# Window attention and a softplus FFN on one core: which block runs while weights are still being converted, and which engine scales the second head

## The chip, the cores and the metric

One core of a Trainium2 chip runs the whole kernel as one program. The metric is the device time of one execution in microseconds (us). The engines of the core work side by side, each through its own instructions in order: TensorE (PE in the profile; PEld is its weight loads), VectorE (DVE), ScalarE (ACT), GpSimd (POOL), and SyncE (SP), which issues all of this kernel's transfers.

## The reference

Eight sequences of 576 tokens, eight heads of 64. Each query sees itself and the 63 tokens before it; the result, 4608 tokens of 512, goes through an FFN with softplus between its two products. All is float32.

```python
scores = scale * np.matmul(q, k.transpose(0, 1, 3, 2))
rel = pos[:, None] - pos[None, :]
scores = np.where((rel >= 0) & (rel < 64), scores, -1e9)
attn = np.exp(scores - np.max(scores, axis=-1, keepdims=True))
attn = attn / (np.sum(attn, axis=-1, keepdims=True) + 1e-09)
x = np.matmul(attn, v)            # heads side by side: 4608 x 512
h = x @ w_in                      # 512 x 2048
g = np.maximum(h, 0.0) + np.log1p(np.exp(-np.abs(h)))
out = g @ w_out                   # 2048 x 512
```

## The kernel before

**Tiling.** The tokens are cut into 12 blocks of 384 (TB), numbered g in the order in which they run (ORDER: first the two blocks that begin a sequence at a block's edge and come first, then the rest). The 2048 middle columns of the FFN are cut into 16 weight tiles f of 128. An FFN *step* is one (g, f): `ffn_up` makes 128 columns of h for the block with 12 matmuls, three ScalarE operations (L454 to L456) and up to three more (L458 to L461) make softplus of it, and `ffn_down` adds its product to the block's three output tiles in ps_o with 9 matmuls. Operands are split into a high and a low float32r part, and each product is made of three.

**Weights.** The weights arrive as float64. `load_w(f)` fetches the two halves of tile f, w_in's and w_out's, and `float64_split` turns the words into a high and a low part: on DVE L162 to L165, on ScalarE L161 and L166, on POOL L167 (and L162 for the first four half tiles). Both parts stay in SBUF for the rest of the run. Tiles 8 to 15 lie in "spare" space that the attention of blocks 0 and 1 uses first.

**Attention.** `attention(g, hp)` handles one pair of heads of one block as a chain of stages, a Python generator. For g < 2 the transposes of q and k are made by TensorE, in float32. For the other blocks q and k are split into bf16 parts in `nat` (L309 to L313), transposed by DMA into `tr` (L314), and multiplied (L334). Then for each 128 tokens come mask and minimum on DVE (L342), exponential with its sum on ScalarE (L345), reciprocal of the sum (L352, L353) and the scaling of the probabilities by it (L358), for both heads; then transposes by TensorE (L379, L380), the product with v (L427) and x, in a high and a low part, in tiles `x{i}_{hp}_{side}`. `nat`, `tr`, `xf` and `vt` exist once, so one pair at a time is in each stage. There are two sets of x tiles: blocks 0 and 1 have one each, and the later blocks take turns, block 2 with the set of block 1.

**Order.** `passes` lists which block runs over which weight tiles: block 0 over tiles 0 to 7 (SPLIT), block 1 over all 16, block 0 over the rest, then each other block over all 16. Where a block stops in between, its sums are written to DRAM (`spill`, the tensor `part`), and when its second pass ends they are fetched and added (`fill`). Everything is put into one list of events, sorted by a number: step n has its first half at 2n + 0.5 and its second at 2n + 3.5, so two units are a step; a pair of heads has its stages at a base plus the offsets in STG0 (blocks 0 and 1), STG2 (block 2) or STG, the base being BASE[g] + PACE[g] * hp for the first three blocks. `load_w(f)` stands 12 units (AHEAD) ahead of the first step that uses f. This list is what the program is traced from. From event 100 on, TensorE's order is that of the list; ahead of it, and on the other engines throughout, a scheduler orders instructions ahead of time, the earlier in the list the sooner where several could go.

Of the kernel before, what the change touches and what calls it, by code (L numbers as in the profile page):

```python
# [8 lines left out]
F32 = mybir.dt.float32  # L9
BF16 = mybir.dt.bfloat16  # L10
F32R = mybir.dt.float32r
U32 = mybir.dt.uint32
AF = mybir.ActivationFunctionType
ALU = mybir.AluOpType

P = 128
TB = 384
# [3 lines left out]

SPLIT = 8
AHEAD = 12
BASE = (-100, -46, 2 * (SPLIT + 16) - 24)
PACE = (5, 5, 4)
STG0 = (-8, 1, 3, 4, 5, 7, 8, 9, 10)
STG2 = (-8, 0, 2, 3, 4, 6, 7, 8, 9)
STG = (-13, -5, 0, 0, 3, 5, 7, 8, 11)
# [8 lines left out]
def window_attention_softplus_ffn(  # L37
# [16 lines left out]
    nc = tc.nc  # L54
    B, H, S, D = q.shape
    NT, DM = out.shape
    DF = w_in.shape[1]
    NP = H // 2
    NC = DM // P
    NF = DF // P  # L60
    NB = NT // TB
# [9 lines left out]
    xp = ctx.enter_context(tc.tile_pool(name="xp", bufs=1))  # L71
    ff = ctx.enter_context(tc.tile_pool(name="ff", bufs=2))
    late = ctx.enter_context(tc.tile_pool(name="late", bufs=1))
    dram = ctx.enter_context(tc.tile_pool(name="dram", bufs=1, space=bass.MemoryType.DRAM))
# [42 lines left out]
    def weight(m, i, f):  # L117

        if f < NE:
            return w_first[m][i][:, f, :]  # L120
        k = (f - NE) // 4
        if (m, i, k) not in w_last:
            w_last[m, i, k] = spare(4 * k + 2 * m + i, [P, 4, DM], F32R, f"w{m}{i}{k}")
        return w_last[m, i, k][:, f % 4, :]
# [19 lines left out]
    def raw_tiles(f):  # L144

        ks = (5,) if f < NE else [k for k in (5,) if k >= 4] if f < NE + 4 else []
        at = f % (len(ks) + 1)
        if at == len(ks):
            return [ff.tile([P, NC, P], w_in.dtype, name="raw", bufs=2) for _ in range(2)]
        t = spare(ks[at], [P, 2, NC, P], w_in.dtype, "raws")  # L150
        return [t[:, m, :, :] for m in range(2)]
# [17 lines left out]
    def load_w(f):  # L169
        fs = slice(f * P, (f + 1) * P)  # L170
        raws = raw_tiles(f)
        for m, src in enumerate((w_in[:, fs].rearrange("(c p) n -> p c n", p=P), w_out[fs, :].rearrange("p (c n) -> p c n", n=P))):
            hi, lo = [weight(m, i, f).rearrange("p (c n) -> p c n", n=P) for i in range(2)]
            float64_split(hi, lo, src, raws[m], 2 * f + m)
# [55 lines left out]
    xs = {}  # L230
    taken_ps = [0]

    def attention(g, hp):
# [6 lines left out]
        def bank():  # L240
            if not odd0:
                return ps_a.tile([P, 512], F32, name="ps_a")

            taken_ps[0] += 1
            return ps_o.tile([P, 512], F32, name=f"ps_o{taken_ps[0] % NJ}")
# [27 lines left out]
        if by_pe:  # L273
# [17 lines left out]
            for hh in range(2):  # L291
                rows = slice(hh * D, (hh + 1) * D)
# [29 lines left out]
        rs = att.tile([P, NJ, 2], F32, name="rs", bufs=2)  # L322
        for j in range(NJ):
            first = j == 0 and not prev
            c0 = WIN if first else 0
            n = W - c0
            sp = bank()
            spv = sp[:, : 2 * n].rearrange("p (h c) -> p h c", h=2)
            kc = slice(j * P + WIN + c0, (j + 2) * P)
            if by_pe:  # L330
                mm(spv, qt[:, j * P : (j + 1) * P], kbd[:, :, j * P + c0 : j * P + W], start=True, stop=True)
            for hh in range(0 if by_pe else 2):
                for i, (a, b) in enumerate(((0, 0), (0, 1), (1, 0))):
                    mm(  # L334
                        spv[:, hh, :], tr_q[a][:, hh, j * P : (j + 1) * P], tr_k[b][:, hh, kc],
                        start=(hh == 0 and i == 0), stop=(hh == 1 and i == 2), skip_group_check=True,
                    )
            t = ORDER[g] * NJ + j
            m = mask_b if (t * P) % S + P > S else mask
            for hh in range(2):  # L340
                pv = p_t[hh][:, j, WIN + c0 :]
                nc.vector.tensor_tensor_reduce(  # L342
                    pv, spv[:, hh, :], m[:, c0:], 1.0, 3.0e38, ALU.add, ALU.min, mn[:, j, hh : hh + 1]
                )
                nc.scalar.activation(  # L345
                    pv, pv, AF.Exp, bias=mn[:, j, hh : hh + 1], scale=-1.0, accum_out=sm[:, j, hh : hh + 1]
                )
            if by_pe and j < NJ - 1:
                yield
                continue  # L350
            jr = slice(0, NJ) if by_pe else slice(j, j + 1)
            nc.vector.tensor_scalar(rs[:, jr, :], sm[:, jr, :], 1.0e-9, None, ALU.add)  # L352
            nc.vector.reciprocal(rs[:, jr, :], rs[:, jr, :])  # L353
            for jj in range(jr.start, jr.stop):
                for hh in range(2):
                    c0 = WIN if jj == 0 and not prev else 0
                    pv = p_t[hh][:, jj, WIN + c0 :]
                    nc.vector.tensor_scalar(pv, pv, rs[:, jj, hh : hh + 1], None, ALU.mult)  # L358
            yield


# [27 lines left out]

        if hp == 0:  # L390
            xs[g] = [[None] * NP, [None] * NP]
        side = 0 if g == 0 else 1 if g == 1 else (g + 1) % 2
        x_t = [xp.tile([P, TB], F32R, name=f"x{i}_{hp}_{side}") for i in range(2)]
        for i in range(2):
            xs[g][i][hp] = x_t[i]
        if by_pe:
# [3 lines left out]
        for hh in range(2):  # L400
# [6 lines left out]
            for kb in reversed(range(NJ)):  # L407
                n = W if kb < NJ - 1 else P
# [26 lines left out]
            yield  # L435


    gs = {}
    ops = {}
    part = {}  # L440
# [23 lines left out]
    def ffn_down(g, f, first, last):  # L464
        gt = gs.pop((g, f))
        if first:
            ops[g] = [ps_o.tile([P, DM], F32, name=f"ps_o{j}") for j in range(NJ)]
        for j in range(NJ):
            js = slice(j * P, (j + 1) * P)
            for i, (a, b) in enumerate(((0, 0), (0, 1), (1, 0))):  # L470
                mm(  # L471
                    ops[g][j], gt[a][:, js], weight(1, b, f),
                    start=(first and i == 0), stop=(last and i == 2),
                )
        if last:
            rows = out[ORDER[g] * TB : (ORDER[g] + 1) * TB, :]
            spill, fill = f < NF - 1, f == NF - 1 and g in part
            if spill:
                part[g] = rows = dram.tile([TB, DM], F32, name="part")
            for j0, j1 in ((0, 2), (2, 3)):  # L480
                o = ff.tile([P, NC, P], w_in.dtype, name="raw", bufs=2).bitcast(F32)
                o = o.rearrange("p c n -> p (c n)").rearrange("p (j n) -> p j n", n=DM)[:, : j1 - j0, :]
                rs = slice(j0 * P, j1 * P)
                if fill:
                    nc.sync.dma_start(o, part[g][rs, :].rearrange("(j p) n -> p j n", p=P))
                for j in range(j0, j1):
                    if fill:
                        nc.vector.tensor_tensor(o[:, j - j0, :], o[:, j - j0, :], ops[g][j], ALU.add)
                    else:
                        (nc.scalar.copy if j == 1 else nc.vector.tensor_copy)(o[:, j - j0, :], ops[g][j])  # L490
                nc.sync.dma_start(rows[rs, :].rearrange("(j p) n -> p j n", p=P), o)
# [2 lines left out]

    passes = [(0, 0, SPLIT), (1, 0, NF), (0, SPLIT, NF)] + [(g, 0, NF) for g in range(2, NB)]
    steps = [(g, f, f == f0, f == f1 - 1) for g, f0, f1 in passes for f in range(f0, f1)]


# [2 lines left out]
    events = []  # L503
    for g in range(NB):
        for hp in range(NP):
            if g < 3:
                base = BASE[g] + PACE[g] * hp
            else:
                base = 2 * NF * (g - 1) + SHP * hp + SH
            stages = attention(g, hp)  # L510
            for at in STG if g >= 3 else STG2 if g >= 2 else STG0:
                events.append((base + at, lambda stages=stages: next(stages, None)))
    loaded = 0
    for n, (g, f, first, last) in enumerate(steps):
        if f == loaded:
            events.append((2 * n - AHEAD, lambda f=f: load_w(f)))
            loaded += 1
        events.append((2 * n + 0.5, lambda g=g, f=f: ffn_up(g, f)))
        events.append((2 * n + 3.5, lambda step=steps[n]: ffn_down(*step)))
    events.sort(key=lambda e: e[0])  # L520
    for at, emit in events:
        if at < PE_ORDERED_FROM:
# [34 lines left out]
```

## Time and profile before

| | us |
|---|---|
| median of 3 runs | 1072.06 (1069.83 to 1072.11) |
| the profiled execution | 1069.74 |
| its span, first to last instruction | 1067.9 |
| PE busy | 1028.4 (96%) |
| DVE busy | 789.0 (74%) |
| ACT busy | 650.0 (61%) |
| POOL busy | 224.7 (21%) |
| mean share of the 16 DMA engines (hardware queue) | 40.0% |
| TensorE clock granted, of full speed | 0.993 |

Each row of the profile's groups stands for all instructions of one source line, engine and operation: count, busy time, mean ns of one, and the idle time of the engine just before them with what ended it. A row of tenths cuts the span into 40 slices of 26.7 us. L358 is line 358 of the kernel before. Busy time of PE is not PE at its peak, since matmuls overlap.

### The profile page before, as it was taken

To read this page: it belongs to the slowest core of one execution; us is meant where nothing else is said; L and a number is where in the kernel's file an instruction comes from. 1 tells how busy PE (TensorE), PEld (TensorE's weight loads), DVE (VectorE), ACT (ScalarE), POOL (GpSimd) and SP (SyncE) were. 2 spreads that over 40 slices of the span, in tenths; PEclk is the share of its full clock that TensorE was granted. 3 is DMA by queue.
4 is the path that set the end of the run, shared out by engine and by line. 5 is a ranking of instruction groups with operands and counts; after the bars stand their busy time and mean duration, and the time that the engine had idled before them with its cause. 6 is when DMAs were issued, how large, how long until landed. Compare 5 with 4: busy or idle time off the path is not lost.

```text
span 1067.9 us, 18172 instructions
## 1 busy us (share of the span) xinstructions
PE 1028.4 (96%) x6096; PEld 924.3 (87%) x6096; DVE 789.0 (74%) x2319; ACT 650.0 (61%) x1669; POOL 224.7 (21%) x217
## 2 busy tenths in 40 slices
PE   7797988999999999999999999999999999999998
PEld 5576867888999899999999999999999999999996
DVE  4999899866777777777777777777777777865433
ACT  6786666666665666566656666656666665655333
POOL 4354355631111111112111111111211111110000
PEclk9999998999999999999999999999999999999999
DMA  7754645255334434343344334424434533520000
GB/s 197 198 140 105 169 105 146 67 127 119 70 71 101 96 79 105 64 97 81 81 96 96 84 76 93 107 60 88 102 74 84 115 80 62 131 51 1 30 1 30
DMA packets 296222, 98.20 MB, mean 92 GB/s; under 512 B 280512, under 2 KB 288704, under 8 KB 296128
## 3 DMA queue, kind: packets, MB, share of 16 engines
q1 hardware_dynamic: 296128, 97.03, 40.0%
q8 instruction: 48, 0.79, 0.3%
q14 instruction: 46, 0.38, 0.1%
HBM read 50.07 MB, written 10.22 MB: 56 GB/s over the span
## 4 chain that ended last, share of the span: by engine, by line
PE 78%; DVE 12%; DMA 4%; ACT 3%; issue 2%; SPq 1%; POOL 0%; DVEq 0%; ACTq 0%
PE ps_h L450 32%; PE ps_o L471 31%; PE ps_a L334 5%; PE ps_a L427 4%; PE ps_a L380 2%; DMA tr<-nat 2%; PE ps_a L379 2%; DVE p_t L358 2%; DVE osb L165 2%; DVE osb L164 1%; DVE osb L162 1%; DVE p_t L342 1%; DVE osb L163 1%; SPq L198 1%; DVE u L458 1%
## 5 line engine op out<-in xcount | busy, mean ns | idle before, releaser
L450 PE MATMUL ps_h<-x,w 128*128 128x384 f32 x2304 | 458.4, 344 | 15.4 <-DVE u L458 11.8
L471 PE MATMUL ps_o<-w,g 128*128 128x512 f32 x1728 | 438.7, 397 | 6.3 <-ACT g L460 4.3
L450 PEld LDWEIGHTS ps_h<-x,w 128*128 128x128 f32 x2304 | 400.6, 189 | 27.5 <-DVE u L458 12.5
L471 PEld LDWEIGHTS ps_o<-w,g 128*128 128x128 f32 x1728 | 318.1, 188 | 65.6 <-ACT g L460 4.6
L458 DVE SCALAR_TENSOR_TENSOR u<-ps_h,u 128x384 f32<-128x384 f32 x192 | 106.0, 552 | 139.7 <-ACT u L456 139.5
L454 ACT ACTIVATE u<-ps_h 128x384 f32<-128x384 f32 x192 | 93.6, 488 | 179.4 <-PE ps_h L450 177.2
L345 ACT ACTIVATE p_t<-p_t,mn 128x192 f32<-128x192 f32 (+1 forms) x288 | 127.0, 443 | 63.5 <-DVE mn L342 63.2
L140 POOL TENSOR_TENSOR x<-xf,x 128x384 fp32r<-128x384 f32 x40 | 41.1, 1027 | 460.6 <-DVE rs L352 362.9
L358 DVE TENSOR_SCALAR p_t<-p_t,rs 128x192 f32<-128x192 f32 (+1 forms) x288 | 110.4, 429 | 2.9
L342 DVE CUSTOM_DVE_ANT_0 p_t<-ps_a,mask 128x192 f32<-128x192 f32 (+1 forms) x244 | 77.3, 343 | 46.5 <-PE ps_a L334 36.1
L455 ACT ACTIVATE u<-u 128x384 f32<-128x384 f32 x192 | 100.7, 526 | 4.1
L456 ACT ACTIVATE u<-u 128x384 f32<-128x384 f32 x192 | 100.6, 524 | 3.2
L461 DVE TENSOR_TENSOR g<-u,g 128x384 fp32r<-128x384 f32 x160 | 89.5, 559 | 3.8 <-DVE g L460 0.5
L385 ACT CAST pt<-ps_a 128x512 fp32r<-128x512 f32 (+1 forms) x144 | 59.0, 417 | 33.7 <-PE ps_a L380 21.9
L312 POOL TENSOR_TENSOR nat<-q_in,nat 128x384 bf16<-128x384 f32 x40 | 38.6, 965 | 187.8 <-ACT nat L311 152.1
L386 DVE TENSOR_TENSOR pt<-ps_a,pt 128x512 fp32r<-128x512 f32 (+1 forms) x144 | 67.9, 477 | 12.3 <-ACT pt L385 10.7
L334 PE MATMUL ps_a<-tr 128*128 128x192 bf16 (+1 forms) x720 | 74.8, 246 | 0.9 <-DVE xf L432 0.7
L460 DVE CAST g<-u 128x384 fp32r<-128x384 f32 x176 | 67.9, 386 | 5.9
L380 PE MATMUL ps_a<-ident,p_t 128*128 128x128 f32 x276 | 66.6, 276 | 1.4 <-DVE p_t L358 1.3
L427 PEld LDWEIGHTS ps_a<-pt,vt 128*128 128x128 f32 (+1 forms) x608 | 64.0, 163 | 3.9 <-issue 0.5
L427 PE MATMUL ps_a<-pt,vt 128*128 128x64 f32 (+4 forms) x608 | 64.5, 247 | 0.4 <-DVE mn L342 0.4
L431 ACT COPY xf<-ps_a 64x384 f32<-64x384 f32 x80 | 38.1, 477 | 40.3 <-PE ps_a L427 37.5
(91 smaller groups left out, 1019.3 us busy)
## 6 DMA issues: line engine op xcount, KB each, us to landing
out_dram<-raw SPq DMA_DIRECT2D x12, 512.0 KB, 3.2
q_in<-in_q_dram SPq DMA_DIRECT2D x56, 96.0 KB, 2.6
raw<-in_moe_w_in_dram SPq DMA_DIRECT2D x10, 512.0 KB, 4.2
raw<-in_moe_w_out_dram SPq DMA_DIRECT2D x10, 512.0 KB, 4.2
k_in<-in_k_dram SPq DMA_DIRECT2D x32, 128.0 KB, 3.5
v_in<-in_v_dram SPq DMA_DIRECT2D x32, 128.0 KB, 2.8
raws<-in_moe_w_in_dram SPq DMA_DIRECT2D x6, 512.0 KB, 4.2
raws<-in_moe_w_out_dram SPq DMA_DIRECT2D x6, 512.0 KB, 5.0
```

Source lines behind the costliest of these rows:

```text
L334: mm(spv[:, hh, :], tr_q[a][:, hh, j * P : (j + 1) * P], tr_k[b][:, hh, kc], start=(hh == 0 and i == 0), stop=(hh == 1 and i == 2), skip_g ...
L342: nc.vector.tensor_tensor_reduce(pv, spv[:, hh, :], m[:, c0:], 1.0, 3.0e38, ALU.add, ALU.min, mn[:, j, hh : hh + 1])
L345: nc.scalar.activation(pv, pv, AF.Exp, bias=mn[:, j, hh : hh + 1], scale=-1.0, accum_out=sm[:, j, hh : hh + 1])
L358: nc.vector.tensor_scalar(pv, pv, rs[:, jj, hh : hh + 1], None, ALU.mult)
L427: mm(av[: D if lo else P, osl], vt[:, vb, hh, : 1 if lo else 2, :], pt[hh][lo][:, psl], start=(i == 0), stop=(i == len(order) - 1), skip_g ...
L450: mm(hv, weight(0, a, f)[:, c * P : (c + 1) * P], x[b][c], start=(i_mm == 0), stop=(i_mm == 3 * NC - 1))
L454: nc.scalar.activation(u, hv, AF.Abs)
L455: nc.scalar.activation(u, u, AF.Exp, scale=-1.0)
L456: nc.scalar.activation(u, u, AF.Ln, bias=1.0)
L458: nc.vector.scalar_tensor_tensor(gf, hv, 0.0, u, ALU.max, ALU.add)
L461: (nc.vector if g >= 2 else nc.gpsimd).tensor_tensor(gt[1], gf, gt[0].bitcast(F32), ALU.subtract)
L471: mm(ops[g][j], gt[a][:, js], weight(1, b, f), start=(first and i == 0), stop=(last and i == 2),)
```

## The change

- `passes` becomes: block 0 over tiles 0 to 7, block 1 over tiles 0 to 7, block 2 over all 16, then block 1 and block 0 over the rest, then blocks 3 to 11.
- Block 2's pairs get the base 8 (was 24), with 4 units between pairs as before; block 3's get an entry of their own, 69 with 5 between (was 59 with 8).
- Weight tiles 8 to 15 are loaded at 10, 14.5, 19 and so on, each 4.5 units on; tiles 0 to 7 as before. Step 24 is the first to use tile 8, step 16 was.
- Every block takes the x tiles of set g % 2, so block 2 takes those of block 0. Block 0's x is copied to DRAM (`keep_x`, at 8.7, behind the start of its first pass) and fetched into tiles of the same set again (`fetch_x`, at 64.7, behind the last step of block 2): 8 transfers of 128x384 float32 each way.
- Block 1 is spilled and filled too.
- The scaling of the second head (L358, `hh` 1) becomes a ScalarE activation (Copy with a scale per partition), in all blocks.

```diff
-BASE = (-100, -46, 2 * (SPLIT + 16) - 24)
-PACE = (5, 5, 4)
+LATE, LATE_PACE = 10, 4.5
+BASE = (-100, -46, 4 * SPLIT - 24, 69)
+PACE = (5, 5, 4, 5)
...
-                    nc.vector.tensor_scalar(pv, pv, rs[:, jj, hh : hh + 1], None, ALU.mult)
+                    if hh:
+                        nc.scalar.activation(pv, pv, AF.Copy, scale=rs[:, jj, hh : hh + 1])
+                    else:
+                        nc.vector.tensor_scalar(pv, pv, rs[:, jj, hh : hh + 1], None, ALU.mult)
...
-        side = 0 if g == 0 else 1 if g == 1 else (g + 1) % 2
-        x_t = [xp.tile([P, TB], F32R, name=f"x{i}_{hp}_{side}") for i in range(2)]
+        x_t = [xp.tile([P, TB], F32R, name=f"x{i}_{hp}_{g % 2}") for i in range(2)]
...
+    x_kept = dram.tile([2 * NP, P, TB], F32, name="x_kept")
+
+    def keep_x():
+        for i in range(2):
+            for hp in range(NP):
+                nc.sync.dma_start(x_kept[i * NP + hp, :, :], xs[0][i][hp].bitcast(F32))
+
+    def fetch_x():
+        xs[0] = [[xp.tile([P, TB], F32R, name=f"x{i}_{hp}_0") for hp in range(NP)] for i in range(2)]
+        for i in range(2):
+            for hp in range(NP):
+                nc.sync.dma_start(xs[0][i][hp].bitcast(F32), x_kept[i * NP + hp, :, :])
...
-                part[g] = rows = dram.tile([TB, DM], F32, name="part")
+                part[g] = rows = dram.tile([TB, DM], F32, name=f"part{g}")
...
-    passes = [(0, 0, SPLIT), (1, 0, NF), (0, SPLIT, NF)] + [(g, 0, NF) for g in range(2, NB)]
+    passes = [(0, 0, SPLIT), (1, 0, SPLIT), (2, 0, NF), (1, SPLIT, NF), (0, SPLIT, NF)]
+    passes += [(g, 0, NF) for g in range(3, NB)]
...
-            if g < 3:
+            if g < len(BASE):
...
         if f == loaded:
-            events.append((2 * n - AHEAD, lambda f=f: load_w(f)))
+            at = 2 * n - AHEAD if f < SPLIT else LATE + LATE_PACE * (f - SPLIT)
+            events.append((at, lambda f=f: load_w(f)))
             loaded += 1
...
+    events.append((SPLIT + 0.7, keep_x))
+    events.append((2 * (2 * SPLIT + NF) + 0.7, fetch_x))
```

## The prediction

> **What bounds the kernel now.** I read the page first, then busy time cut at the starts of the FFN blocks, then the line that marks an FFN step.
>
> ```profile
> span 1067.9 us, 18172 instructions
> PE 1028.4 (96%) x6096; PEld 924.3 (87%) x6096; DVE 789.0 (74%) x2319; ACT 650.0 (61%) x1669; POOL 224.7 (21%) x217
> PE   7797988999999999999999999999999999999998
> DVE  4999899866777777777777777777777777865433
> PEclk9999998999999999999999999999999999999999
> PE 78%; DVE 12%; DMA 4%; ACT 3%; issue 2%; SPq 1%; POOL 0%; DVEq 0%; ACTq 0%
> ```
>
> PE's row of tenths is full from the ninth slice to the end; only the first eight (each 26.7 us) have holes, and there DVE is full. The chain's 12% on DVE must lie there. So the kernel has a head bound by DVE and a body bound by PE. L454 is the first ScalarE operation behind each FFN step's first matmuls, once per step, so its count and first and last start date the steps. Five stretches of 16, 16, 16, 128 and 16 steps:
>
> ```profile
> L454 ACT ACTIVATE u<-ps_h x16: 468/483/495, 53.4 to 149.5; 128x384 f32<-128x384 f32 x16
> L454 ACT ACTIVATE u<-ps_h x16: 469/492/497, 159.1 to 244.3; 128x384 f32<-128x384 f32 x16
> L454 ACT ACTIVATE u<-ps_h x16: 472/492/493, 249.6 to 328.0; 128x384 f32<-128x384 f32 x16
> L454 ACT ACTIVATE u<-ps_h x128: 468/492/504, 334.6 to 991.5; 128x384 f32<-128x384 f32 x128
> L454 ACT ACTIVATE u<-ps_h x16: 492/492/493, 995.7 to 1058.2; 128x384 f32<-128x384 f32 x16
> ```
>
> And the busy time of the engines between those starts (columns: PE, PEld, DVE, ACT, POOL, TensorE clock, DMA share, GB/s; 211.3 is where the chain leaves DVE for good):
>
> ```profile
> 0.00:53.40 53.40, 40.31 (x196) 29.49 (x197) 39.94 (x138) 36.29 (x106) 22.18 (x31) 0.97 0.74 197
> 53.40:105.00 51.60, 43.82 (x225) 36.23 (x224) 50.80 (x118) 39.67 (x103) 24.75 (x20) 0.97 0.50 127
> 105.00:159.10 54.10, 48.03 (x270) 40.63 (x270) 48.94 (x110) 32.69 (x79) 26.54 (x20) 1.00 0.50 132
> 159.10:211.30 52.20, 45.40 (x250) 39.89 (x250) 47.84 (x111) 33.97 (x83) 29.04 (x23) 0.93 0.43 110
> 211.30:249.60 38.30, 38.30 (x233) 34.52 (x230) 23.40 (x69) 24.70 (x63) 12.73 (x13) 1.00 0.51 116
> 249.60:334.60 85.00, 85.00 (x525) 77.02 (x524) 62.70 (x195) 49.93 (x135) 12.53 (x12) 1.00 0.41 88
> 334.60:995.70 661.10, 660.43 (x4078) 606.93 (x4077) 489.15 (x1532) 406.94 (x1057) 96.99 (x100) 1.00 0.39 83
> ```
>
> PE loses 13.1 + 7.8 + 6.1 + 6.8 = 33.8 us up to 211.3 and next to nothing behind it; DVE is busy for 147.6 of the 157.9 us from 53.4 to 211.3 (93%). The last 16 steps run without attention beside them, 62.5 us for 15, so a step is 4.17 us of PE and a block 66.7. The 128 steps of the body take 661.1 us, 82.6 a block, so a block's attention is about 16 us of PE. Nothing in the body can be won by what the diff does, and whatever it brings shows in when step 48 (block 3's first) starts, now 334.6 us.
>
> **The change part by part.** Block 2's 16 steps move ahead of the late halves of blocks 1 and 0. Step 16 now needs all of block 2's attention and only weight tiles 0 to 7; before, it needed no block 2 attention but tile 8 at once. Tile 8 is now due at step 24. From step 16 on PE then has 32 steps, 133 us, plus block 3's attention, 16 us: 149 us up to step 48, if nothing stalls it. So the sum is: when does step 16 start? Before it starts at 159.1, and PE then needs 175.5 us to step 48, because weights and block 2's attention still hold it.
>
> DVE is the bound up to there, 139.7 us busy of 159.1 (three windows above). Its costliest groups in 0 to 159.1 (columns: busy, mean ns):
>
> ```profile
> L358 DVE TENSOR_SCALAR p_t<-p_t,rs 128x192 f32<-128x192 f32 (+1 forms) x58 | 25.3, 499 | 0.2
> L163 DVE TENSOR_SCALAR osb<-osb 128x512 uint32<-128x512 uint32 x25 | 16.9, 677 | 0.9 <-POOL osb L162 0.7
> L162 DVE TENSOR_SCALAR osb<-osb 128x512 f32<-128x512 f32 x21 | 11.2, 534 | 4.3 <-ACT osb L161 4.3
> L165 DVE SCALAR_TENSOR_TENSOR osb<-raw,osb 128x512 uint32<-128x512 uint32 x13 | 10.9, 835 | 0.0
> L164 DVE SCALAR_TENSOR_TENSOR osb<-raws,osb 128x512 uint32<-128x512 uint32 x12 | 10.8, 897 | 0.2
> L165 DVE SCALAR_TENSOR_TENSOR osb<-raws,osb 128x512 uint32<-128x512 uint32 x12 | 10.6, 884 | 0.1
> L164 DVE SCALAR_TENSOR_TENSOR osb<-raw,osb 128x512 uint32<-128x512 uint32 x13 | 10.4, 800 | 0.1
> ```
>
> 1. *Scaling of the second head.* Half of the 58 leave DVE: 12.7 us of the 25.3. Price on ScalarE, and how a scaling reads with less around it:
>
> ```profile
> L358 DVE TENSOR_SCALAR p_t<-p_t,rs x58: 274/310/1404, 14.7 to 154.6; 128x192 f32<-128x192 f32 x42, 128x128 f32<-128x128 f32 x16
> L358 DVE TENSOR_SCALAR p_t<-p_t,rs x144: 278/315/978, 405.4 to 890.1; 128x192 f32<-128x192 f32 x128, 128x128 f32<-128x128 f32 x16
> L345 ACT ACTIVATE p_t<-p_t,mn x144: 386/447/459, 403.0 to 888.0; 128x192 f32<-128x192 f32 x128, 128x128 f32<-128x128 f32 x16
> ```
>
> No ScalarE scaling is in the trace; the nearest is L345, same tile and shape, 447 ns, which I take (from 0 to that: 0 to 13 us). 29 of them are 13 us on a ScalarE that is 108.7 us busy of 159.1, 68%, so 76%. In the body 12 a block are 5.4 us on 50.9 of 82.6; PE has no idle there, and the change in DVE and ACT is worth nothing in it. The scalings' mean of 499 ns against a median of 310, with single ones at 1404, says that many wait for something inside the instruction. The Trainium skill, SBUF — State Buffer, section "Who interferes with whom", has it that a DVE operation in a two-port mode and a GpSimd operation shut each other out for a whole instruction; POOL is 73.5 us busy of 159.1 here, and the trace agrees with the spread. By that rule the move is worth the 12.7 us, and without it 29 x 0.31 = 9.0.
>
> 2. *Weights.* By 159.1 DVE had done 25 half tiles, 12.5 tiles, for 70.8 us (the six rows under L358), 5.66 us a tile. In the new order tiles 0 to 7 and five late ones (at 10, 14.5, 19, 23.5 and 28) are issued ahead of step 16 at 32.5: 13 tiles, +2.8 us. Bounds: 8 tiles, -25 us, if the late ones wait; 16, +20 us, if they fill every gap. I take 13, since tile 12.5 was in fact in front of step 16 when the order issued 15. The rest, 17 us, falls into the 33 us of steps 16 to 23 and costs nothing.
>
> 3. *Block 2's attention* must be issued 16 units of the list sooner (its last stage at 29, not 45, ahead of step 16 at 32.5). Of the 58 scalings by 159.1, 48 belong to the eight head pairs of blocks 0 and 1, so 10 to block 2, 1.7 pairs of six; with the conversions for the next, some 2.1 of its four pairs were done and 1.9 come on top. What a pair costs DVE I take from the body, by way of the FFN's own operations:
>
> ```profile
> L458 DVE SCALAR_TENSOR_TENSOR u<-ps_h,u 128x384 f32<-128x384 f32 x192 | 106.0, 552 | 139.7 <-ACT u L456 139.5
> L461 DVE TENSOR_TENSOR g<-u,g 128x384 fp32r<-128x384 f32 x160 | 89.5, 559 | 3.8 <-DVE g L460 0.5
> L460 DVE CAST g<-u 128x384 fp32r<-128x384 f32 x176 | 67.9, 386 | 5.9
> ```
>
> 489.15 / 8 = 61.1 a block, less 16 x 1.50 = 24 for these three and some 2 for the eviction, leaves 35, 8.8 a pair; less three scalings at 0.315 it is 7.9; in the crowded head nearer 9. So +17 (15 to 19).
>
> 4. *x spilled and fetched, a second spill and fill.* 16 transfers of 128x384 f32 (197 KB) and four of the spilled sums. One issue in the chain of waits:
>
> ```profile
> 61.66 0.60 SPq L198
> ```
>
> So some 12 us of SP in 250, and 3.1 MB of x and 1.6 MB of sums against a DMA share of 0.5 or less from 53.4 on. The copy out waits for nothing, since block 0's x is complete when step 0 runs; behind it in SP's queue stand loads for block 2 and weights, 5 us late at worst. The fetch waits for step 31's matmuls and is due at step 40, 8 steps or 33 us later; what it holds up in SP's queue is block 3's loads and transposes, issued five or more units (10 us) ahead of their use. A fill lies before in 249.6 to 334.6, where PE has no hole, so the second should be hidden by block 0's first matmuls. I take 2 us for the whole part (0 to 8).
>
> 5. *Last link.* From the last scaling to x lie transposes, two evictions, products and the split. The list leaves 3.5 units, nearly two steps, for them; with DVE full they come late: 2 us (0 to 8).
>
> Sum for step 16: 159.1 - 12.7 + 2.8 + 17 + 2 = 168. Step 48: 168 + 149 + 2 = 319, against 334.6: 15.5 us less. The profiled execution took 1069.7 us (span 1067.9), 2.3 below the median of the runs, 1072.1. From the one I get 1054.2, from the other 1056.6; I say 1056. A measurement here can tell about 0.2%, 2 us.
>
> **The rivals.**
>
> *A, slower: block 2's attention is held by its own chain, not by DVE's total.* One pair uses tr, nat and xf at a time.
>
> ```profile
> L309 ACT ACTIVATE nat<-q_in x5: 523/525/527, 63.9 to 186.5; 128x384 bf16<-128x384 f32 x5
> L334 PE MATMUL ps_a<-tr x77: 242/246/368, 106.0 to 230.0; 128*128 128x192 bf16 x77
> ...
> DMA to landing us min/median/max: 3.8/4.9/7.8
> ...
> 204.05 0.34 DVE L139 CAST x<-xf 128x384 fp32r<-128x384 f32 x1
> 205.52 0.48 ACT L431 COPY xf<-ps_a 64x384 f32<-64x384 f32 x1 [1.39 <-POOL x L140]
> ```
>
> Five pairs (block 2's four and the next) take their first conversion between 63.9 and 186.5: 30.7 us apart. If that pace stays, scores of the first pair at 106 less 12.7, three more pairs, and five units (2.5 steps, 10.4 us) from scores to x: 93.3 + 92 + 10.4 = 196. Step 48 at 345, 10.5 us late: 1080 to 1083. It decides from a step 16 behind 184 us, that is a pace over 26.7. For it: DVE stays full, each link of the chain queues in it, and the transposes take 3.8 to 7.8 us to land. Against: the slow pace was partly by order (block 2 stood behind the late weights) and partly by its x tiles, which were block 1's and came free only around 204 (the first cast into x is at 204.05, and xf's next writer waits for the split of it). Now they are block 0's, free after step 7 (around 100). The Trainium skill, TensorE: Matmul & The Clock Gate, section "What's actually happening", says that an idle PE falls to half its clock after some 3.4 us; in this rival the wait at step 16 would add a few us by it. The rows show 0.93 in 159.1 to 211.3, not a half over long.
>
> *B, much faster: late weights give way.* With 8 to 9 tiles ahead of step 16, DVE would be through by 168 - 25 = 143, or 149, and PE, idle for 27 us up to 159.1 and with some 9 us of attention more, needs about 141. Step 48 at 294 to 300, 1031 to 1038. Against: DVE does what is ready, and weights nearly always are.
>
> *C, nothing: each gain is given back.* Step 16 at about 184 by a mix of A and 16 tiles ahead, or ScalarE at 76% becoming late in the weights' casts and the FFN's three operations: 1070 to 1074.
>
> **How the numbers follow.** The sum's case (step 16 from 158 to 179, 1046 to 1068) has 0.62; B and what lies between, 0.12; C 0.09; A 0.17. The likeliest is 1056. For eight in ten the range takes in C, what lies between the sum and B, and the edge of A: 1040 to 1077. Faster by over 0.2%: 0.62 + 0.12 + 0.03 of C's edge, 0.77; the same 0.06; slower 0.17.
>
> **What would show it.** Right: L454's 17th start near 168, and from there to the 49th about 150 us with PE full; DVE full to about 168 and not to 211; L358 halved with as many ScalarE operations near 0.4 us; block 3's first step near 319, and from there to the end 733 us as before. Wrong: a hole on PE before the 17th start with DVE not full (A); DVE's groups of L162 to L165 all done ahead of step 16 (C), or only nine tiles (B); PE waiting for weights' casts at the 25th step; holes in the body with ScalarE as releaser; SP standing before the fetch while block 3's loads queue behind it.

## The result and the profile after

The changed kernel takes 1086.0 us (1085.2 to 1088.1) against 1070.9: a ratio of 1.0145, 95% interval 1.0122 to 1.0168. Forecast were 1056 and a gain; it is a loss of 15 us, and the range ended at 1077. Rival A, priced at 1080 to 1083, comes nearest: it has step 16 at 196 us, and it came at 196.3.

The page of the changed kernel:

```profile
span 1084.2 us, 18308 instructions
PE 1033.2 (95%) x6096; PEld 929.0 (86%) x6096; DVE 754.8 (70%) x2178; ACT 701.5 (65%) x1813; POOL 221.6 (20%) x217
PE   6787787899999999999999999999999999999998
DVE  4999999965354767767767776766776766765433
PEclk9999899899999999999999999999999999999999
PE 80%; DVE 12%; ACT 2%; DMA 2%; issue 2%; SPq 1%; POOL 0%; DVEq 0%; ACTq 0%
```

The body looks as before; DVE has 34 us less and ScalarE 52 more; the head still has its eight slices with holes. The first ScalarE operation of a step, now L471, dates the steps again (stretches of 16, 16, 16 and 144):

```profile
L471 ACT ACTIVATE u<-ps_h x16: 466/476/496, 49.9 to 164.2; 128x384 f32<-128x384 f32 x16
L471 ACT ACTIVATE u<-ps_h x16: 470/491/492, 196.3 to 269.6; 128x384 f32<-128x384 f32 x16
L471 ACT ACTIVATE u<-ps_h x16: 472/492/494, 274.4 to 343.4; 128x384 f32<-128x384 f32 x16
L471 ACT ACTIVATE u<-ps_h x144: 469/492/503, 350.1 to 1074.8; 128x384 f32<-128x384 f32 x144
```

Step 15 comes at 164.2 and step 16 not before 196.3: a hole of 32 us between two steps, where the kernel before went on at 159.1. Step 48 starts at 350.1 (334.6 before), and from there to the end it is 734 us, as before (733). So the 15.5 us are all in the head. Busy time in the head (same columns as in the prediction):

```profile
0.00:49.90 49.90, 33.59 (x181) 26.32 (x181) 33.34 (x115) 39.18 (x115) 21.91 (x31) 1.00 0.81 215
49.90:103.20 53.30, 44.71 (x230) 37.16 (x229) 51.47 (x116) 43.53 (x115) 26.11 (x21) 0.97 0.64 168
103.20:164.20 61.00, 51.58 (x296) 44.76 (x295) 59.11 (x140) 42.49 (x111) 28.79 (x23) 0.89 0.60 139
164.20:196.30 32.10, 21.76 (x133) 17.27 (x132) 29.58 (x88) 21.33 (x61) 12.75 (x11) 0.91 0.72 164
196.30:274.40 78.10, 77.17 (x431) 68.62 (x431) 54.40 (x149) 47.20 (x123) 11.72 (x10) 0.95 0.39 90
```

Over the whole span TensorE stands for 51.0 us (39.5 before) and is busy for 1033.2 us (1028.4 before) with as many matmuls, 6096: some 12 us of the loss are standing, and some 5 are matmuls that take longer (granted clock 0.986, before 0.993).

And the tiles that step 16 waits for: the first scores of block 2 (L335 on `tr`) and the casts that complete its x, one a pair (L140):

```profile
L335 PE MATMUL ps_a<-tr x96: 242/246/383, 107.2 to 199.6; 128*128 128x192 bf16 x96
...
L140 DVE CAST x<-xf x4: 339/348/352, 145.5 to 193.3; 128x384 fp32r<-128x384 f32 x4
```

Block 2's pairs begin to score at 107, its x comes at 145.5, 171.0, 183.1 and 193.3, and step 16 runs 3 us behind the last. TensorE had done its first 16 steps by then. In the hole it is busy for 21.8 of 32.1 us, with the rest of step 15, with attention, and with steps 16 and 17 as far as the pairs of x had come; their last six matmuls wait for the last pair, and it had no step of another block to run meanwhile. (TensorE's order follows the list only from position 100 on, which is step 50; in the head the scheduler orders it too.)

### The profile page after: what moved, and what is told of

It is laid out like the page before. It is cut to its first block, busy times and chain, and to the rows that moved or that the text cites. A ratio compares the mean times of both kernels' runs of the same rounds, so it can differ in the third digit from the quotient of the medians.

```text
span 1084.2 us, 18308 instructions
## 1 busy us (share of the span) xinstructions
PE 1033.2 (95%) x6096; PEld 929.0 (86%) x6096; DVE 754.8 (70%) x2178; ACT 701.5 (65%) x1813; POOL 221.6 (20%) x217
## 4 chain that ended last, share of the span: by engine, by line
PE 80%; DVE 12%; ACT 2%; DMA 2%; issue 2%; SPq 1%; POOL 0%; DVEq 0%; ACTq 0%
PE ps_h L467 33%; PE ps_o L488 33%; PE ps_a L335 5%; PE ps_a L430 4%; PE ps_a L384 2%; PE ps_a L383 2%; DVE osb L165 2%; DMA tr<-nat 1%; DVE p_t L343 1%; DVE osb L163 1%; DVE osb L166 1%; DVE osb L164 1%; DVE p_t L362 1%; ACT p_t L346 1%; DVE u L475 1%
## 5 line engine op out<-in xcount | busy, mean ns | idle before, releaser
L471 ACT ACTIVATE u<-ps_h 128x384 f32<-128x384 f32 x192 | 93.4, 488 | 161.3 <-PE ps_h L467 160.1
L141 POOL TENSOR_TENSOR x<-xf,x 128x384 fp32r<-128x384 f32 x40 | 41.7, 1043 | 434.4 <-DVE rs L353 363.5
L360 ACT ACTIVATE p_t<-p_t,rs 128x192 f32<-128x192 f32 (+1 forms) x144 | 62.2, 444 | 26.1 <-DVE rs L354 22.8
L313 POOL TENSOR_TENSOR nat<-q_in,nat 128x384 bf16<-128x384 f32 x40 | 38.5, 963 | 196.3 <-ACT nat L312 166.0
L335 PE MATMUL ps_a<-tr 128*128 128x192 bf16 (+1 forms) x720 | 75.1, 248 | 0.9 <-DVE xf L435 0.9
L362 DVE TENSOR_SCALAR p_t<-p_t,rs 128x192 f32<-128x192 f32 (+1 forms) x144 | 70.0, 496 | 2.6
L383 PE MATMUL ps_a<-ident,p_t 128*128 128x128 f32 x248 | 62.8, 282 | 8.3 <-DVE p_t L362 7.7
L384 PE MATMUL ps_a<-ident,p_t 128*128 128x128 f32 x276 | 67.8, 281 | 2.1 <-DVE mn L343 1.0
```

Of the source, the lines that this page charges most:

```text
L335: mm(spv[:, hh, :], tr_q[a][:, hh, j * P : (j + 1) * P], tr_k[b][:, hh, kc], start=(hh == 0 and i == 0), stop=(hh == 1 and i == 2), skip_g ...
L384: tp(pp[:, j * W : j * W + P], p_t[hh][:, j, P:], ident)
L471: nc.scalar.activation(u, hv, AF.Abs)
```

## The experiments

The two theories: T1, step 16 waits for DVE's volume, in whose order late weight tiles stand between block 2's links; T2, for the chain of block 2's pairs, whatever DVE has to do. Times are medians; the kernel before ran at 1069.8 to 1070.5 beside them.

**1. The two parts of the change, each alone.** The new order with both heads on DVE:

```diff
-                    if hh:
-                        nc.scalar.activation(pv, pv, AF.Copy, scale=rs[:, jj, hh : hh + 1])
-                    else:
-                        nc.vector.tensor_scalar(pv, pv, rs[:, jj, hh : hh + 1], None, ALU.mult)
+                    nc.vector.tensor_scalar(pv, pv, rs[:, jj, hh : hh + 1], None, ALU.mult)
```

> The new order of blocks, weights and x copies, with both heads scaled on DVE as before. In the changed kernel step 16 starts at 196.3 us and step 48 at 350.1; 36 scalings had left DVE ahead of step 16, at 0.47 us each 17 us. Theory T1 (step 16 waits for DVE's work in DVE's order, in which weight tiles 8 and up stand between block 2's links): DVE is full, so the 17 us come back, step 16 at about 210, 1098 to 1103 us. Theory T2 (the chain of one pair of heads at a time sets the pace, 20.8 us a pair, whatever else DVE has to do): only the chain's own scalings get longer, 1086 to 1091. If the ScalarE scaling itself does the harm: faster than 1086.

1097.0 us, 1.0256 (1.0241 to 1.0272). The order costs 26 us, and the scaling takes 11 of them back. Step 16:

```profile
L468 ACT ACTIVATE u<-ps_h x16: 471/492/494, 205.5 to 280.2; 128x384 f32<-128x384 f32 x16
```

It is 9 us later than with the moved scaling. The time is just under T1's range and 6 us over T2's. The scaling alone, in the old order:

> The kernel before with the second head's scaling on ScalarE and nothing else. If DVE's total is what bounds the head: the 34 scalings of the second head up to 211 us leave DVE at 0.47 us each, 16 us, of which 10 or more show: 1055 to 1061. If the freed time is filled by weight tiles that nobody waits for yet: 1068 to 1072. If ScalarE becomes late: over 1073.

1072.7 us, 1.0018 (1.0008 to 1.0029): no gain, a trace of a loss. The trace is of the quickest of the ten runs, 1068.9, nearly 4 us under their median. Steps 16 to 31 and 32 to 47 against 159.1 and 249.6 before, and one of the weights' operations on DVE, before and with the scaling moved:

```profile
L457 ACT ACTIVATE u<-ps_h x16: 473/492/494, 156.8 to 243.2; 128x384 f32<-128x384 f32 x16
L457 ACT ACTIVATE u<-ps_h x16: 473/492/497, 248.6 to 327.3; 128x384 f32<-128x384 f32 x16
```

```profile
L163 DVE TENSOR_SCALAR osb<-osb x25: 411/423/1276, 21.3 to 156.2; 128x512 uint32<-128x512 uint32 x25
```

```profile
L163 DVE TENSOR_SCALAR osb<-osb x27: 415/637/1528, 20.7 to 159.0; 128x512 uint32<-128x512 uint32 x27
```

Two us at step 16 are one at step 32. The scalings on DVE take 13.7 us up to 211.3 in place of 32.0, but DVE's busy time falls only from 187.5 to 178.9 us: L163's median rises from 423 to 637 ns (its mean from 677 to 804), so part of the waiting inside the instruction has moved to other operations, and what is really free turns into idle time. So 8.6 us less on a DVE that is 93% busy did not help the old head. ScalarE is busy for 14.3 us more up to there (156.9 against 142.6); whether that took a gain back, this run does not tell.

**2. Late weights later, block 2 earlier.**

```diff
-LATE, LATE_PACE = 10, 4.5
+LATE, LATE_PACE = 30, 2.5
```

> The changed kernel with weight tiles 8 to 15 listed at 30, 32.5, ... 47.5 in place of 10, 14.5, ... 41.5; step 16 is at 32.5, step 24 (first to use tile 8) at 48.5. T1: 30 half tiles are done by DVE ahead of step 16 in the changed kernel, 2.83 us each; with some 20, step 16 starts 15 to 28 us sooner, at 170 to 181, and if tile 8 is in time for step 24, 1058 to 1072. T2: the pace of the pairs stays near 21 us, step 16 at 190 or later, 1080 to 1090. A third way: step 16 is sooner, but step 24 waits for tile 8, and the sum stays at about 1086.

1084.8 us, 1.0145 (1.0127 to 1.0163), as the changed kernel. Steps 16 to 23 and 24 to 31:

```profile
L471 ACT ACTIVATE u<-ps_h x8: 468/489/492, 186.9 to 226.6; 128x384 f32<-128x384 f32 x8
L471 ACT ACTIVATE u<-ps_h x8: 468/490/493, 233.3 to 268.5; 128x384 f32<-128x384 f32 x8
```

Step 16 is 9.4 us sooner, between the two theories. Step 24, the first to use a late tile, is still 4.6 us sooner (237.9 in the changed kernel), and step 32 only 1.0 (273.4 against 274.4): as in the third way the gain is lost to late tiles, but little by little, while DVE converts them beside block 2's steps (busy for 51.8 of 53.1 us from 186.9 to 240, against 43.5). Step 48 comes at 347.8. The other edit:

```diff
-BASE = (-100, -46, 4 * SPLIT - 24, 69)
+BASE = (-100, -46, 4 * SPLIT - 36, 69)
```

> The changed kernel with block 2's pairs listed 12 units sooner (base -4 in place of 8). T1: its links come ahead of more weight tiles (0 to 7 too) on DVE, but those are needed for steps 4 to 15: steps 8 to 15 later, step 16 at 185 to 195, 1076 to 1086. T2: the chain starts sooner by up to 12 units at some 6 us each step, limited by x tiles that come free behind step 7 (103 us): step 16 at 175 to 185, 1066 to 1076.

1085.5 us, 1.0144 (1.0129 to 1.0159); block 2's x comes from 145.6 to 192.5, as without it, and step 16 at 194.7. T2 had 1066 to 1076 and missed; the time lies in T1's range. Block 2's place in the list isn't what makes it late.

**3. No late tiles at all, then fewer early ones.** In `weight()`, steps over 7 use tile f - 8, so the kernel leaves out half of the weights:

```diff
+        f = f % NE
...
-        if f == loaded:
+        if f == loaded and f < SPLIT:
```

> The changed kernel without the conversion of weight tiles 8 to 15: steps with f over 7 use tile f - 8 in their place, so that DVE loses 14 half tiles (40 us) ahead of step 16 and nothing waits for a late tile; every other instruction stays. T1 (DVE's volume in its order holds step 16): step 16 at 155 to 168, step 48 at 305 to 318, 1040 to 1055. T2 (the chain of pairs holds it, whatever DVE has to do): with tiles listed later the pairs came 18.4 us apart and step 16 started at 186.9; here step 16 at 178 to 187, step 48 at 328 to 338, 1063 to 1074.

1067.7 us, 0.9971 (0.9961 to 0.9980), in T2's range. Steps 16 to 31, and the busy time ahead of them:

```profile
L472 ACT ACTIVATE u<-ps_h x16: 468/491/492, 178.5 to 252.6; 128x384 f32<-128x384 f32 x16
```

```profile
105.00:159.10 54.10, 50.56 (x331) 45.14 (x330) 39.57 (x130) 38.20 (x109) 17.72 (x17) 1.00 0.52 102
159.10:185.00 25.90, 16.08 (x96) 13.64 (x95) 18.50 (x60) 16.54 (x45) 4.79 (x5) 0.79 0.70 141
```

The late tiles are worth 17.8 us of step 16's delay. Without them DVE is busy for 39.6 of 54.1 and 18.5 of 25.9 us and TensorE still stands for 10 us from 159.1 to 185: even with some 40 us less on DVE step 16 did not come at 168. The tiles take time on ScalarE, GpSimd and the DMA queue as well, so the 17.8 us are not shown to be DVE's alone. On top of that, tiles 4 to 7 left out:

```diff
-        f = f % NE
+        f = f % 4
...
-        if f == loaded and f < SPLIT:
+        if f == loaded and f < 4:
```

> The kernel without the late tiles, now with tiles 4 to 7 left out as well (steps use tile f modulo 4): eight half tiles, 23 us of DVE, less ahead of 100 us. Block 2's first scores come at 106 to 112 us in all kernels so far, where block 1's attention ends. If DVE's volume ahead of it (attention of blocks 0 and 1 and tiles 0 to 7) sets that: first scores at 85 to 92, step 16 at 150 to 165, 1040 to 1055. If the pairs of blocks 0 and 1 have a pace of their own (11 us a pair from 8.5 us on): first scores at 100 or later, step 16 at 170 or later, 1060 to 1068.

1064.4 us, 0.9946 (0.9926 to 0.9965).

```profile
50.00:105.00 55.00, 53.49 (x300) 47.05 (x299) 28.58 (x93) 38.33 (x106) 14.73 (x14) 0.98 0.20 43
```

```profile
L472 ACT ACTIVATE u<-ps_h x16: 467/490/492, 175.9 to 247.0; 128x384 f32<-128x384 f32 x16
```

23 us less on DVE, which is now half idle from 50 to 105, bring 2.6 us; first scores at 103. In this run TensorE is full there (53.5 of 55): steps and the attention of block 1 share it, and block 2's pairs come behind.

**4. What paces the pairs.** Without the late tiles, and with more room:

```diff
-            tr = att.tile([P, NT2, P], BF16, name="tr")
-            nat = att.tile([P, NT2, 2, D], BF16, name="nat")
+            tr = att.tile([P, NT2, P], BF16, name="tr", bufs=2)
+            nat = att.tile([P, NT2, 2, D], BF16, name="nat", bufs=2)
...
-            xf = att.tile([P, TB], F32, name="xf")
+            xf = att.tile([P, TB], F32, name="xf", bufs=2)
```

> The kernel without the late tiles (as in the run with tile f - 8 in their place), with nat, tr and xf twice each, in the room that the late tiles leave: two pairs of block 2 can be in conversion, transpose and products at a time. If the single buffers set the pace of the pairs: pairs under 15 us apart, step 16 10 us or more sooner than without the second set. If it is the chip's engines in the order given (DVE, TensorE's order behind block 1's attention): within 3 us of the run without the second set.

1063.8 us, 0.9938 (0.9923 to 0.9953). Step 16:

```profile
L472 ACT ACTIVATE u<-ps_h x16: 470/491/494, 176.4 to 251.4; 128x384 f32<-128x384 f32 x16
```

2.1 us sooner; the rest of the gain comes behind step 16. The conversions run ahead, the rest of the chain is hardly faster. Without the late tiles, at least, rival A's reason (one `nat`, `tr` and `xf`) is not it. With less for TensorE instead, one of the three products in both halves of block 1's steps:

```diff
+            ab = ((0, 0), (0, 1), (1, 0))[: 1 if g == 1 else 3]
```

> The kernel without the late tiles, and block 1's 16 steps with one of the three products each (7 matmuls in place of 21): 22 us less for TensorE ahead of step 16 (steps 8 to 15) and 22 us less behind it (steps 32 to 39). Neither a second set of nat, tr and xf nor 23 us less for DVE moved step 16 much; what is left is TensorE's order, in which the stages of block 2's pairs stand between half steps, or the length of one pair's chain itself. TensorE's order: pairs 4 to 6 us closer together, step 16 at 155 to 165. The pair's own chain (mask, exponential, sum, scaling, transposes, products, one behind the other over four engines): step 16 at 172 to 179, and the total 22 us under the 1067.7 of that run, from steps 32 to 39 alone: 1043 to 1047.

1052.2 us, 0.9832 (0.9815 to 0.9848). Step 16 comes between the two readings; the total is over the second one's 1043 to 1047:

```profile
L473 ACT ACTIVATE u<-ps_h x16: 469/490/493, 170.9 to 244.4; 128x384 f32<-128x384 f32 x16
```

22 us less for TensorE make step 16 7.6 us sooner: TensorE's work has a share, and two thirds of the 22 do not show there. With steps 32 to 39 cut short too, step 48 comes 21 us sooner (311.5 against 332.5), and 5 of these are lost again behind it; why, was not followed. What else sets the 11 to 21 us from one pair's first scores to the next's (the chain of one pair over four engines, the single `vt` and `pt`, three banks of ps_a) was not separated.

**5. The copies of x left out.** Block 0's second pass takes block 2's x in their place:

```diff
-    events.append((SPLIT + 0.7, keep_x))
-    events.append((2 * (2 * SPLIT + NF) + 0.7, fetch_x))
+    events.append((2 * (2 * SPLIT + NF) + 0.7, lambda: xs.update({0: xs[2]})))
```

> The changed kernel without the 16 copies of block 0's x: block 0's second pass takes block 2's x in their place. If the copies are hidden, as forecast (2 us with the second fill): 1083 to 1087. If they hold SP's queue and with it block 2's loads and transposes: step 16 five or more us sooner, below 1081.

1085.5 us, 1.0139 (1.0121 to 1.0157): hidden.

**6. Filling the hole.**

```diff
-    passes = [(0, 0, SPLIT), (1, 0, SPLIT), (2, 0, NF), (1, SPLIT, NF), (0, SPLIT, NF)]
+    passes = [(0, 0, SPLIT), (1, 0, SPLIT + 4), (2, 0, NF), (1, SPLIT + 4, NF), (0, SPLIT, NF)]
...
-    events.append((2 * (2 * SPLIT + NF) + 0.7, fetch_x))
+    events.append((2 * (2 * SPLIT + 4 + NF) + 0.7, fetch_x))
```

> The changed kernel with block 1's first pass over 12 tiles and its second over the last four, so that block 2 comes in at step 20. If the loss is PE standing in front of a block 2 that is ready at about 196 us whatever PE does: four steps (17 us of PE work) fill the hole from 164 to 196, step 48 at 333 to 336, 1068 to 1072. If the four steps wait for tiles 8 to 11 or take DVE from the chain: block 2 later, 1078 to 1090.

1077.3 us, 1.0065 (1.0048 to 1.0082), just under the second reading and 5 us over the first.

```profile
L471 ACT ACTIVATE u<-ps_h x16: 467/492/498, 168.4 to 257.8; 128x384 f32<-128x384 f32 x16
```

Step 16 runs at 168.4 now and belongs to block 1; block 2 starts at 202.0, 6 us later than in the changed kernel, with four more steps done. Step 48 comes at 340.9: nine of the 17 us of work come back. It is the best of the complete kernels in the new order, and no match for the kernel before.

**7. A third work tile for the weights**, in the old order, first beside the moved scaling, then alone:

```diff
-        w = ff.tile([P, NC, P], F32, name="osb", bufs=2)
+        w = ff.tile([P, NC, P], F32, name="osb", bufs=3)
```

> The order before, second head on ScalarE, and a third buffer for osb, the work tile of a half tile's conversion. With the scaling moved alone DVE had 18% idle from 105 to 159 us and 13% from 159 to 211, and the weights still came 6.2 us a half tile. If two osb buffers hold that pace (a half tile is some 6 us from fetch to the last subtraction): tile 15 ready 10 to 25 us sooner than 196.5, 1055 to 1066. If it is the order of the engines' other work: 1069 to 1074.

> The kernel before with the third buffer for osb alone. DVE is full there, so a third half tile in flight finds no room: 1068 to 1073; if it helps as much as beside the moved scaling, the buffer was the limit and not DVE.

1080.6 us (1.0104, 1.0087 to 1.0121) and 1082.0 us (1.0117, 1.0100 to 1.0135): slower by 1%, which neither expectation had. Casts of the weights up to 105 us and block 1's last x, before and with three tiles alone:

```profile
L166 ACT CAST w<-osb x16: 602/620/624, 24.2 to 104.9; 128x512 fp32r<-128x512 f32 x16
...
L422 DVE TENSOR_TENSOR x<-ps_a,x x6: 545/545/558, 20.0 to 111.0; 128x384 fp32r<-128x384 f32 x6
```

```profile
L166 ACT CAST w<-osb x17: 600/618/642, 23.7 to 99.2; 128x512 fp32r<-128x512 f32 x17
...
L422 DVE TENSOR_TENSOR x<-ps_a,x x6: 530/547/558, 19.0 to 120.1; 128x384 fp32r<-128x384 f32 x6
```

The weights run some 8 to 10 us ahead (the 16th cast at 95.1) and the attention of block 1 ends 9 us later. Up to 105 us DVE spends 47.8 us on the weights (L162 to L165) and has done 42 scalings; in the kernel before it is 43.9 us and 48. Step 8, block 1's first, follows the last x by some 2 to 3 us in both (at 122.4, before at 113.9), and step 16 comes at 172.1, 13 us later. So with the same work for DVE, more weights in flight meant a later attention, and step 8 waits for that.

## Why the prediction was wrong

**The method failed, at the sum for step 16.** "DVE is the bound up to there", and so I added and took away DVE time, to 168 us; step 16 came at 196.3. The scaling alone, in the old order, moved it by 2.3 us in the quickest run where 12.7 were counted, and some 63 us less weight work on DVE, from the changed kernel to the run with four tiles, moved it by 20.4. What step 16 waits for is block 2's chain: it begins to score at 103 to 111 us in all runs of the new order, whether DVE is 97% or 52% busy from 50 to 105. From there to the last x it takes 78 to 94 us with the late tiles and 62 to 70 without. The order with both heads on DVE, and the run with four tiles:

```profile
L335 PE MATMUL ps_a<-tr x102: 242/246/383, 111.2 to 211.8; 128*128 128x192 bf16 x102
...
L140 DVE CAST x<-xf x4: 346/349/354, 150.9 to 202.4; 128x384 fp32r<-128x384 f32 x4
```

```profile
L336 PE MATMUL ps_a<-tr x108: 243/246/383, 102.6 to 209.7; 128*128 128x192 bf16 x108
...
L141 DVE CAST x<-xf x4: 346/350/354, 128.8 to 172.5; 128x384 fp32r<-128x384 f32 x4
```

**Block 2's attention (item 3)** was the step that failed: it was priced as +17 us of DVE, where its links, waiting for each other, made step 16 late by the whole rest of the chain, 86 us from its first scores to its last x. I had seen that its pairs came 30.7 us apart in the kernel before and put that down to order and x tiles. There TensorE had steps 16 to 31 to run while the pairs came through; the new order takes this cover away, and the prediction did not say what would hide a late pair.

**Weights (item 2)**: counted were 13 tiles ahead of step 16; 15 had been begun.

```profile
L164 DVE TENSOR_SCALAR osb<-osb x30: 405/427/1495, 22.4 to 195.1; 128x512 uint32<-128x512 uint32 x30
```

That is an error of two tiles in the count, 11 us at the sum's price. But a sum of DVE time does not hold here either way: leaving out all late tiles, some 40 us of DVE, was worth 17.8 us. This is T1's part of the truth; T2's is that 178.5 remain without them. What sets the pace of the pairs then stays open.

**Rival A** gave 196 us for step 16, and it came at 196.3, though not by its working: first scores come at 107 us for 93, the fourth pair's 60 us later for 92, and step 16 another 29 us later for 10. That the sums meet is luck. It said that a PE hole would show "with DVE not full"; DVE was busy for 29.6 of the 32.1 us of the hole, with late weights and block 3's first conversions. The chance of 0.17 looks too low: the pace of the pairs was the one row that bore directly on what step 16 newly waits for.

**Right**: the time from step 16 to step 48 (153.8 against 149 + 2); the body unchanged (734 us against 733) with the scaling on ScalarE; the price of that scaling (447 ns taken); the copies hidden, and the fills, whose additions (L505) lie from 313.1 to 356.0, where PE has no hole.

```profile
L360 ACT ACTIVATE p_t<-p_t,rs x144: 386/452/460, 14.1 to 989.8; 128x192 f32<-128x192 f32 x128, 128x128 f32<-128x128 f32 x16
...
L505 DVE TENSOR_TENSOR raw<-raw,ps_o x6: 670/680/689, 313.1 to 356.0; 128x512 f32<-128x512 f32 x6
...
274.40:350.10 75.70, 75.70 (x426) 68.27 (x425) 33.93 (x87) 43.06 (x100) 23.79 (x23) 1.00 0.33 82
350.10:1012.30 662.20, 661.60 (x4080) 607.04 (x4079) 466.82 (x1435) 439.00 (x1146) 96.50 (x100) 1.00 0.39 83
```

## What to carry to other kernels

An engine that is 93% busy is the bound of a stretch only if taking work from it moves the end of the stretch; test that with the cheapest part of a change alone before summing its time. Where a change lets a stage be needed sooner, follow that stage's own chain from its first link to its last at the pace the trace shows, and ask what work the waiting engine has left meanwhile. More background work in flight (here a third work tile) can delay a chain on the same engines although the work as a whole is no more.

## What the runs showed of the hardware

Where TensorE has stood, its granted clock falls:

```profile
120.00:130.00 10.00, 6.70 (x25) 5.91 (x26) 10.00 (x26) 7.98 (x21) 4.91 (x5) 0.55 0.44 132
190.00:200.00 10.00, 5.69 (x27) 3.71 (x24) 10.00 (x32) 7.94 (x27) 3.90 (x3) 0.69 1.09 197
200.00:210.00 10.00, 10.00 (x46) 9.10 (x47) 10.00 (x29) 7.98 (x23) 3.60 (x3) 0.80 0.53 144
```

From 200 to 210 TensorE is busy throughout at 0.80 of its clock. Cut into single microseconds the clock is 0.50 from 194 to 204, though TensorE is busy throughout from 198 on, and 0.97 to 1.00 from 204 on: by an estimate from these figures some 3 us of the 154 from step 16 to step 48. The Trainium skill, TensorE: Matmul & The Clock Gate, section "What's actually happening", has idle TensorE at half clock until it has been busy for some 3.4 us. The trace agrees on the half; busy throughout, TensorE stayed at it for some 6 us here.

The Trainium skill, Perfetto Trace Analysis, section "Optimizing Scalar/DVE Operations", says that moving work from a saturated DVE to ScalarE may make sense. Here it was worth 11 us in the order where block 2's attention held TensorE up, and nothing (1.0018) in the other, at much the same 93 to 97% of DVE: the share of busy time did not tell the two apart.
